# Turning the keys of batches 2 and 3 by 32x32 block transposes and an exchange through DRAM

## The chip, the core and the metric

The kernel runs on one core of one Trainium2 chip. The metric is the device time of one execution in microseconds (us). Three executions of the kernel before took 861.26 to 861.43 us, with a median of 861.28 us.

## What is computed

A linear attention feeds two pairs of dense layers. All arrays are fp32; there are 4 batches, 8 heads, 576 positions and 64 channels a head, so 2304 tokens of 512 channels, and 2048 hidden channels in each of the two layers.

```python
q_s = softmax of q over the channels of a head      # (4, 8, 576, 64)
k_s = softmax of k over the 576 positions
kv  = np.einsum('bhsd,bhse->bhde', k_s, v)          # 64 x 64 per head
x   = np.einsum('bhsd,bhde->bhse', q_s, kv)         # -> (2304, 512)
h   = x @ moe_w_in;   x = elu(h) @ moe_w_out
h   = x @ moe2_w_in;  out = (h * tanh(softplus(h))) @ moe2_w_out
```

The sum over positions in `kv` does not depend on the order of the positions, as long as K and V are in the same order.

## The kernel before

Matrix products are made of three fp32r products of high and low parts, so that a step of the first layer has 12 matmuls for the hidden channels (`mm_h`, L409) and 12 for the output (`mm_y`, L458). The 2304 tokens are 18 tiles of 128, worked through in five blocks `j` of 4, 3, 4, 3 and 4 tiles; a block has 16 **slots** `f`, one for each 128 of the hidden channels. In a slot TensorE does `mm_h(j, f)` and then `mm_y` of two slots before; ScalarE and VectorE make the ELU and the split into parts in between. A block of 3 tiles has matmuls of 384 columns, one of 4 tiles has 512.

The attention of the next tokens is laid beside these slots, by a table of entries `at(j, f, where, function)`. Within a slot the places stand in a fixed order: "load" (DMA issues), the ELU's exponentials, "mid", the ELU's join on VectorE, then "pe" (on TensorE that is right behind `mm_h` and ahead of `mm_y`), "post", "last" and "late". Every engine, and every DMA queue, works through its own instructions in the order of this table; an instruction that waits holds up all behind it on the same engine. Nearly all loads go through the queue of SyncE (SP), stores of split weights through GpSimd's (POOL).

`kv_chain(j, f, b)` (from L606) places the keys and values of batch `b`, four pairs `hp` of heads, each pair at slot `s = f + 2 hp`. Batch 1 runs beside block 0, batch 2 beside block 1 and batch 3 beside block 2; for the latter two `f` is -1, so pairs 0 to 3 have s = -1, 1, 3 and 5. For a pair: `load_k` fetches K with the 128 channels of the pair on the partitions and 576 positions along them (L218); `k_max` (VectorE, L241) and `k_exp` (ScalarE, L248) make the exponentials in place. For `kv` the positions have to lie on the partitions. `k_turn` does this with four 128x128 transposes on TensorE (L263), `k_turn_rest` with one for the last 64 positions (L280); `k_turned` and `k_turned_rest` copy them out of PSUM with ScalarE (L268, L286). `load_v` fetches V (L225, and L229 for the last 64 rows) into one buffer that all pairs share, `k_kv` multiplies (L297; five chunks of positions, two heads each), and `k_scale` writes the result, divided by the sums, into `kvbd`. There it is used by `q_x` (L369) for the query tiles, which are prepared in the same way by `q_chain`.

Three buffers hold K (tag `kT`); the third query tile of a block borrows one. A DMA on SP's queue also waits for the eighth DMA ahead of it, since eight completion counters are used in turn.

Of the kernel before, what the change touches and what calls it, by code (L numbers as in the profile page):

```python
# [8 lines left out]
F32 = mybir.dt.float32  # L9
# [7 lines left out]
P = 128  # L17
# [23 lines left out]
def attention_elu_mish(  # L41
# [15 lines left out]
    nc = tc.nc  # L57
    B, DM, S = kT.shape
    NT = q.shape[0]
    DFF = w1_in.shape[1]  # L60
    D = 64
    NHP = DM // P
# [18 lines left out]
    NC = (S + P - 1) // P  # L81
# [6 lines left out]
    dram = ctx.enter_context(tc.tile_pool(name="dram", bufs=1, space=bass.MemoryType.DRAM))  # L88
# [117 lines left out]
    km_t, qm_t, kv_t, turn_t, x_t = {}, {}, {}, {}, {}  # L206
# [14 lines left out]
    def load_v(b, hp, t=None):  # L221
        if t is None:
            t = ap.tile([P, NC, P], F32, tag="v", name="v", bufs=1)
        full = S // P
        nc.sync.dma_start(  # L225
            out=t[:, 0:full, :], in_=v[b, hp, 0:full * P, :].rearrange("(c p) e -> p c e", p=P)
        )
        if S % P:
            nc.sync.dma_start(out=t[0:S % P, full, :], in_=v[b, hp, full * P:S, :])  # L229
            nc.gpsimd.memset(t[S % P:P, full, :], 0.0)  # L230
        v_t[b, hp] = t
# [19 lines left out]
    def inverse(s):  # L251
        nc.vector.tensor_scalar(out=s, in0=s, scalar1=EPS, scalar2=None, op0=ALU.add)
        nc.vector.reciprocal(out=s, in_=s)
# [34 lines left out]
            )  # L288

    def k_kv(b, hp, ps=None):  # L290
        e, vv = en_t.pop((b, hp)), v_t.pop((b, hp))
        if ps is None:
            ps = att_psum()
        for c in range(NC):

            for a in (0, D):
                nc.tensor.matmul(  # L297
                    out=ps[a:a + D, a:a + D], lhsT=e[:, c, a:a + D], rhs=vv[:, c, a:a + D],
                    start=(c == 0), stop=(c == NC - 1),
                )  # L300
        kv_t[b, hp] = ps

    def k_scale(b, hp, engine=None):
        ps, r = kv_t.pop((b, hp)), rk_t.pop((b, hp))
        for h in range(2):
            a, z = h * D, (h + 1) * D
            to, by = kvbd[b % 2][a:z, hp, a:z], r[a:z, :]
            if engine is None:
                nc.scalar.activation(out=to, in_=ps[a:z, a:z], func=AF.Copy, scale=by)
            else:  # L310
                engine.tensor_scalar(
                    out=to, in0=ps[a:z, a:z], scalar1=by, scalar2=None, op0=ALU.mult
                )

    NH = DM // D

# [281 lines left out]
    def at(j, f, where, fn, *a):  # L598
        j, f = j + f // NF, f % NF
        beside.setdefault((j, f, where), []).append((fn, a))  # L600
# [5 lines left out]
    def kv_chain(j, f, b):  # L606
        for hp in range(NHP):

            s = f + 2 * hp
            if j or hp > 2:  # L610
                at(j, s - 2, "load", load_k, b, hp)
            if (b, hp) not in v_t:
                at(j, s + 2, "load", load_v, b, hp)
            at(j, s, "late", k_max, b, hp)
            at(j, s, "late", k_exp, b, hp)
            at(j, s + 2, "post", lambda b, hp: inverse(rk_t[b, hp]), b, hp)
            at(j, s + 3, "post", k_scale, b, hp)


            rest = s + 1 if j else s + 2  # L620
            if j and hp:
                at(j, s + 1, "pe", k_kv, b, hp - 1)
            at(j, rest, "pe", k_turn_rest, b, hp)
            at(j, rest, "pe", k_turned_rest, b, hp)
            if not j or hp == NHP - 1:
                at(j, s + 3, "pe", k_kv, b, hp)
            at(j, s + 1, "pe", k_turn, b, hp)
            at(j, s + 1, "pe", k_turned, b, hp)

# [271 lines left out]
```

## Time and profile before

| | |
|---|---|
| median of three executions | 861.28 us (861.26 to 861.43) |
| span of the profiled execution, first to last instruction | 859.0 us |
| time outside that span, against the median | 2.3 us |
| TensorE busy (matmuls) | 849.1 us, 99% of the span |
| VectorE / ScalarE / GpSimd busy | 587.7 / 456.4 / 160.6 us |
| DMA, mean over the span | 114 GB/s |

The profiled execution is known by its span alone: its own time is not among the three. Busy time of TensorE is not work at peak, since matmuls overlap; the pace of the starts in the timeline tells what one costs. The whole stretch that the change touches lies between about 120 and 260 us, beside blocks 1 and 2.

### The profile page before, as it was taken

Reading aid. Unit: us, or ns where it says so; the run is one execution under the profiler, and the core shown is the slowest. Engines: PE = TensorE matmul, PEld = TensorE weight load, DVE = VectorE, ACT = ScalarE, POOL = GpSimd, SP = SyncE. Lnnn points to the kernel's source line nnn. Section 1 sums busy time; section 2 is a strip of 40 time slices with the busy share of each in tenths; the row PEclk is TensorE's granted clock in tenths of the full one; section 3 lists DMA queues with packets and bytes.
Section 4 is the critical chain, followed back from the end, with each engine's and each line's share of the span. In section 5 each row is a group of like instructions: output and inputs, shape, how many; then the busy total and the mean of one; then the engine's idle time right before and its main releaser. Section 6 shows DMA issues by size and latency. Waiting matters only on the chain.

```text
span 859.0 us, 11796 instructions
## 1 busy us (share of the span) xinstructions
PE 849.1 (99%) x4408; PEld 734.4 (86%) x4408; DVE 587.7 (68%) x1040; ACT 456.4 (53%) x865; POOL 160.6 (19%) x210
## 2 busy tenths in 40 slices
PE   8999999999999999999999999999999999999998
PEld 5778889998888899988889998888888888888996
DVE  7899856655455367444446878777777777777776
ACT  7897757656554465544444544444444444444443
POOL 4365623223211233223332000000000000000000
PEclk9999999999999999999999999999999999999999
DMA  9791547553643374437977003100210021000101
GB/s 307 244 320 51 185 128 262 163 152 97 215 137 98 112 220 117 136 104 235 290 238 266 1 1 98 38 1 1 98 50 1 1 74 50 1 1 0 50 1 38
DMA packets 55050, 98.30 MB, mean 114 GB/s; under 512 B 3920, under 2 KB 32848, under 8 KB 52432
## 3 DMA queue, kind: packets, MB, share of 16 engines
q1 hardware_dynamic: 38720, 52.31, 19.8%
q0 software_dynamic: 16128, 45.09, 16.0%
q8 instruction: 35, 0.57, 0.3%
q14 instruction: 23, 0.19, 0.1%
q10 hardware_dynamic: 144, 0.13, 0.0%
HBM read 70.25 MB, written 27.26 MB: 114 GB/s over the span
## 4 chain that ended last, share of the span: by engine, by line
PE 95%; ACT 1%; issue 1%; POOL 1%; DVE 1%; DMA 0%; SPq 0%; POOLq 0%; ACTq 0%
PE h L409 44%; PE y L458 23%; PE y L546 15%; PE a L546 8%; PE a L369 2%; PE a L297 1%; PE a L355 1%; PE a L263 1%; DMA q<-in_q_dram 0%; POOL wil L186 0%; PE a L280 0%; DVE qs L340 0%; ACT early L148 0%; ACT woh L180 0%; POOL wol L186 0%
## 5 line engine op out<-in xcount | busy, mean ns | idle before, releaser
L424 DVE SCALAR_TENSOR_TENSOR e<-h,e 128x512 f32<-128x512 f32 (+1 forms) x80 | 50.9, 637 | 116.9 <-ACT e L420 116.5
L409 PE MATMUL h<-xha,wih 128*128 128x512 f32 (+1 forms) x328 | 125.1, 385 | 0.7 <-ACT xha L385 0.7
L409 PE MATMUL h<-xla,wih 128*128 128x512 f32 (+1 forms) x328 | 125.3, 385 | 0.5 <-DVE xla L389 0.5
L409 PE MATMUL h<-xha,wil 128*128 128x512 f32 (+1 forms) x328 | 125.3, 385 | 0.3 <-POOL wil L186 0.3
L514 ACT ACTIVATE r<-n,two 128x512 f32<-128x512 f32 (+1 forms) x80 | 54.6, 683 | 131.3 <-DVE n L510 131.3
L458 PE MATMUL y<-gh,wol 128*128 128x512 f32 (+1 forms) x320 | 120.7, 379 | 0.3 <-POOL wol L186 0.3
L458 PE MATMUL y<-gh,woh 128*128 128x512 f32 (+1 forms) x320 | 117.5, 369 | 0.0
L458 PE MATMUL y<-gl,woh 128*128 128x512 f32 (+1 forms) x320 | 117.4, 368 | 0.0
L416 ACT ACTIVATE e<-h 128x512 f32<-128x512 f32 (+1 forms) x80 | 44.5, 556 | 119.4 <-PE h L409 119.4
L409 PE MATMUL h<-xhb,wih 128*128 128x384 f32 (+1 forms) x304 | 104.8, 345 | 0.0
L409 PE MATMUL h<-xhb,wil 128*128 128x384 f32 (+1 forms) x304 | 104.7, 344 | 0.0
L409 PE MATMUL h<-xlb,wih 128*128 128x384 f32 (+1 forms) x304 | 104.6, 344 | 0.0
L186 POOL TENSOR_TENSOR lo<-raw,hi 128x512 fp32r<-128x512 f32 x32 | 44.2, 1380 | 234.1 <-ACT hi L180 130.9
L493 ACT ACTIVATE u<-h 128x512 f32<-128x512 f32 (+1 forms) x80 | 44.1, 552 | 71.6 <-PE h L409 71.6
L503 DVE TENSOR_SCALAR u<-u 128x512 f32<-128x512 f32 (+1 forms) x80 | 32.0, 400 | 65.0 <-ACT u L493 65.0
L442 DVE TENSOR_TENSOR gl<-e,gh 128x512 fp32r<-128x512 f32 (+1 forms) x80 | 52.5, 656 | 33.6 <-ACT gh L438 33.5
L546 PE MATMUL y<-woh,gl 128*128 128x512 f32 x192 | 75.3, 392 | 0.0
L546 PE MATMUL y<-woh,gh 128*128 128x512 f32 x192 | 75.2, 391 | 0.0
L546 PE MATMUL y<-wol,gh 128*128 128x512 f32 x192 | 74.8, 389 | 0.0
L409 PEld LDWEIGHTS h<-xha,wih 128*128 128x128 f32 x328 | 61.1, 188 | 13.1 <-ACT xha L385 0.9
L409 PEld LDWEIGHTS h<-xha,wil 128*128 128x128 f32 x328 | 61.2, 188 | 12.8 <-POOL wil L186 0.8
L409 PEld LDWEIGHTS h<-xla,wih 128*128 128x128 f32 x328 | 61.2, 188 | 12.6 <-DVE xla L389 0.7
(164 smaller groups left out, 1749.0 us busy)
## 6 DMA issues: line engine op xcount, KB each, us to landing
raw<-in_moe_w_out_dram SPq DMA_DIRECT2D x23, 512.0 KB, 4.7
raw<-in_moe_w_in_dram SPq DMA_DIRECT2D x21, 512.0 KB, 5.0
early<-in_moe_w_in_dram SPq DMA_DIRECT2D x11, 512.0 KB, 5.9
early<-in_moe_w_out_dram SPq DMA_DIRECT2D x9, 512.0 KB, 6.4
out_dram<-o SPq DMA_DIRECT2D x17, 256.0 KB, 2.3
w2ih<-hi POOLq DMA_DIRECT2D x16, 256.0 KB, 4.8
w2il<-lo POOLq DMA_DIRECT2D x16, 256.0 KB, 5.2
w2oh<-hi POOLq DMA_DIRECT2D x16, 256.0 KB, 5.1
```

Of the source, the lines that this page charges most:

```text
L186: nc.gpsimd.tensor_tensor(out=lo, in0=z, in1=hi.bitcast(F32), op=ALU.subtract)
L263: nc.tensor.transpose(out=ps[:, c], in_=k_t[b, hp][:, c], identity=ident)
L369: nc.tensor.matmul(out=ps[:, hp, t0:t1], lhsT=kvbd[b % 2][:, hp, :], rhs=u[:, hp, t0:t1], start=True, stop=True,)
L409: nc.tensor.matmul(out=h_t[f][:, c], lhsT=w[:, i, k * P:(k + 1) * P], rhs=x[k][:, c], start=(n == 0), stop=(n == 3 * KD - 1),)
L416: nc.scalar.activation(out=e, in_=h_t[f], func=AF.Exp)
L424: nc.vector.scalar_tensor_tensor(out=e, in0=h_t[f], scalar=0.0, in1=e, op0=ALU.max, op1=ALU.subtract)
L442: nc.vector.tensor_tensor(out=gl_t[f], in0=h_t.pop(f), in1=gh_t[f].bitcast(F32), op=ALU.subtract)
L458: nc.tensor.matmul(out=y_t[e][:, 0:gh.shape[1]], lhsT=w[:, i, e * P:(e + 1) * P], rhs=x, start=(f == 0 and n == 0), stop=(f == NF - 1 and ...
L493: nc.scalar.activation(out=u, in_=h_t[f], func=AF.Exp)
L503: nc.vector.tensor_scalar(out=u, in0=u, scalar1=U_MAX, scalar2=None, op0=ALU.min)
L514: nc.scalar.activation(out=r, in_=n, func=AF.Ln, bias=two)
L546: nc.tensor.matmul(out=y_t[p, t], lhsT=x[:, c], rhs=w[:, i, :], start=(f == 0 and n == 0), stop=(f == NF - 1 and n == 2),)
```

## The change

For batches 2 and 3 (`b > 1`, that is j = 1 and 2 in `kv_chain`) the transposes on TensorE and the copies on ScalarE are gone. In their place the exponentials are written to DRAM as they lie (`k_out`, one DMA of 128 runs of 2304 bytes) and read back by `k_in` in another arrangement: four DMAs to 32 partitions each, in runs of 512 bytes, and two in runs of 128 bytes for the last 64 positions. In the new arrangement each 32x32 block has its channels on the partitions, and blocks that belong to one range of positions share a partition group; VectorE then transposes all blocks in place (`k_blocks`, two instructions, 128x4x4x32 and 128x128). After it a partition holds four neighbouring positions instead of positions 128 apart, so V is read in the same order ("(p c) e": 128 runs of 2048 bytes instead of 512 runs of 512). `k_kv` reads the turned K with its 64 channels 16 bytes apart for four of its five chunks (`k_heads`). The slots of the table move: `load_v` from s+2 to s+4, `k_kv` from s+3 (where the next pair's entry is at its s+1) to s+5, `k_scale` from s+3 to s+5. The batches 0 and 1 are untouched.

```diff
@@ load_v
+        rows = "(p c) e -> p c e" if b > 1 else "(c p) e -> p c e"
         nc.sync.dma_start(
-            out=t[:, 0:full, :], in_=v[b, hp, 0:full * P, :].rearrange("(c p) e -> p c e", p=P)
+            out=t[:, 0:full, :], in_=v[b, hp, 0:full * P, :].rearrange(rows, p=P)
         )
@@ k_kv
-                    out=ps[a:a + D, a:a + D], lhsT=e[:, c, a:a + D], rhs=vv[:, c, a:a + D],
-                    start=(c == 0), stop=(c == NC - 1),
+                    out=ps[a:a + D, a:a + D],
+                    lhsT=k_heads(b, hp, c, a) if b > 1 else en_t[b, hp][:, c, a:a + D],
+                    rhs=vv[:, c, a:a + D], start=(c == 0), stop=(c == NC - 1),
                 )
@@ new functions
+    R = 32
+
+    def k_out(b, hp):
+        d = dram.tile([P, S], F32, name=f"turn_k{b}{hp}")
+        nc.sync.dma_start(out=d, in_=k_t[b, hp])
+        turn_t[b, hp] = d
+
+    def k_in(b, hp):
+
+        t, n = en_t[b, hp].rearrange("p c e -> p (c e)"), S // P * P
+        d = turn_t.pop((b, hp)).rearrange("(a j) s -> j a s", j=R)
+        for to, size, first in ((t[:, 0:n], P, 0), (t[:, n:n + P], R, n)):
+            for r in range((S - first) // size if first else P // R):
+                nc.sync.dma_start(
+                    out=to[r * R:(r + 1) * R, :].rearrange("j (a s) -> j a s", s=size),
+                    in_=d[:, :, first + r * size:first + (r + 1) * size],
+                )
+
+    def k_blocks(b, hp):
+        t, n = en_t[b, hp].rearrange("p c e -> p (c e)"), S // P * P
+        for x in (t[:, 0:n].rearrange("p (a i c) -> p a c i", i=R, c=n // P), t[:, n:n + P]):
+            nc.vector.transpose(out=x, in_=x)
+
+    def k_heads(b, hp, c, a):
+        t, n = en_t[b, hp].rearrange("p c e -> p (c e)"), S // P
+        if c < n:
+            t = t[:, 0:n * P].rearrange("p (a j c) -> p c a j", j=R, c=n)[:, c]
+        else:
+            t = t[:, n * P:].rearrange("p (a j) -> p a j", j=R)
+        return t[:, a // R:(a + D) // R, :]
@@ kv_chain
-                at(j, s + 2, "load", load_v, b, hp)
+                at(j, s + (4 if j else 2), "load", load_v, b, hp)
@@
+            if j:
+                at(j, s + 1, "late", k_out, b, hp)
+                at(j, s + 2, "late", k_in, b, hp)
+                at(j, s + 4, "post", k_blocks, b, hp)
+                at(j, s + 5, "pe", k_kv, b, hp)
+                at(j, s + 5, "post", k_scale, b, hp)
+                continue
             at(j, s + 3, "post", k_scale, b, hp)
-            rest = s + 1 if j else s + 2
-            if j and hp:
-                at(j, s + 1, "pe", k_kv, b, hp - 1)
-            at(j, rest, "pe", k_turn_rest, b, hp)
-            at(j, rest, "pe", k_turned_rest, b, hp)
-            if not j or hp == NHP - 1:
-                at(j, s + 3, "pe", k_kv, b, hp)
+            at(j, s + 2, "pe", k_turn_rest, b, hp)
+            at(j, s + 2, "pe", k_turned_rest, b, hp)
+            at(j, s + 3, "pe", k_kv, b, hp)
```

The order that the table gives is seen best at two places. (Line numbers in the rows of the change are those of the changed file: L298 there is L297 here, L443 is L409, L492 is L458, L226 and L230 are L225 and L229, L237 is L236.) First TensorE in block 1, slot 2, between `mm_h` and `mm_y`; `xhb` is the block's input, `kT` the buffer of K, `ident` the identity of a transpose. Before:

```order
L409 MATMUL h<-xhb,wih 128x384
L297 MATMUL a<-v,kT 64x64 x10
L280 MATMUL a<-ident,kT 64x128
L263 MATMUL a<-ident,kT 128x128 x4
L458 MATMUL y_1492<-gh,wol 128x384
```

Of the change, in slot 4, where the same product of pair 0 stands now:

```order
L443 MATMUL h<-xhb,wih 128x384
L298 MATMUL a<-v,kT 64x64 x10
L492 MATMUL y_1468<-gh,wol 128x384
```

The product of a pair stays; the turn of the next pair that stood behind it is gone, and the product stands two slots later.

The second place is SP's queue beside block 1, from the load of V for pair 1 on. Before (the first load of V is that of pair 1, `kT<-in_kT_dram` is K of pair 3):

```order
L225 DMA v<-in_v_dram 128x4x128
L229 DMA v<-in_v_dram 64x128
L218 DMA kT<-in_kT_dram 128x576
L133 DMA raw<-in_moe_w_out_dram 128x1024
L236 DMA q<-in_q_dram 128x512
L225 DMA v<-in_v_dram 128x4x128
```

Of the change, from K of pair 3 to the load of V for pair 1 (`turn_k_1464` is the exchange of pair 1, `turn_k_1587` that of pair 2):

```order
L218 DMA kT<-in_kT_dram 128x576
L331 DMA kT<-turn_k_1464 32x4x128 x4
L331 DMA kT<-turn_k_1464 32x4x32 x2
L133 DMA raw<-in_moe_w_out_dram 128x1024
L322 DMA turn_k_1587<-kT 128x576
L237 DMA q<-in_q_dram 128x512
L226 DMA v<-in_v_dram 128x512
L230 DMA v<-in_v_dram 64x128
```

V of pair 1 was the first DMA behind the product of pair 0 and is now the tenth; K of pair 3, which waits for that same product (its buffer is the one that pair 0 leaves), stands ahead of all the others.

## Rows read from the trace of the kernel before

**Rows 1.** The page: the span, and the busy time of each engine.
```profile
span 859.0 us, 11796 instructions
...
PE 849.1 (99%) x4408; PEld 734.4 (86%) x4408; DVE 587.7 (68%) x1040; ACT 456.4 (53%) x865; POOL 160.6 (19%) x210
```

**Rows 2.** The page: the chain that ended last, by engine.
```profile
PE 95%; ACT 1%; issue 1%; POOL 1%; DVE 1%; DMA 0%; SPq 0%; POOLq 0%; ACTq 0%
```

**Rows 3.** Timeline of TensorE, turn of pair 0; columns: start, us, what, records merged.
```profile
121.30 0.27 PE L280 MATMUL a<-ident,kT 128*64 128x128 f32 x1
121.40 0.60 PE L263 MATMUL a<-ident,kT 128*128 128x128 f32 x4
121.76 0.47 PE L458 MATMUL y<-gh,wol 128*128 128x512 f32 x1
122.07 0.39 PE L458 MATMUL y<-gl,woh 128*128 128x512 f32 x1
```

**Rows 4.** Timeline of TensorE, product of pair 0 and turn of pair 1.
```profile
131.67 0.80 PE L297 MATMUL a<-v,kT 128*64 128x64 f32 x20
132.41 0.30 PE L280 MATMUL a<-ident,kT 128*64 128x128 f32 x1
132.54 0.60 PE L263 MATMUL a<-ident,kT 128*128 128x128 f32 x4
132.90 0.42 PE L458 MATMUL y<-gh,wol 128*128 128x384 f32 x1
```

**Rows 5.** Groups of TensorE by form, 118 to 302 us: count, busy us, mean ns.
```profile
L297 PE MATMUL a<-v,kT 128*64 128x64 f32 x160 | 6.4, 227 | 0.0
...
L263 PE MATMUL a<-ident,kT 128*128 128x128 f32 x32 | 4.8, 273 | 0.0
...
L280 PE MATMUL a<-ident,kT 128*64 128x128 f32 x8 | 2.3, 292 | 0.0
```

**Rows 6.** Timeline of TensorE, fp32 products of the query tiles.
```profile
157.13 1.05 PE L369 MATMUL a<-q,kvbd 128*128 128x128 f32 x8
...
279.61 1.89 PE L369 MATMUL a<-kT,kvbd 128*128 128x64 f32 x16
281.31 0.48 PE L458 MATMUL y<-gh,wol 128*128 128x512 f32 x1
```

**Rows 7.** Groups of ScalarE, 118 to 262 us: every other word read, and all.
```profile
L180 ACT ACTIVATE hi<-raw 128x512 fp32r<-128x512 f32 x13 | 8.5, 654 | 0.0
...
L336 ACT ACTIVATE q<-q 128x512 f32<-128x512 f32 x5 | 3.1, 615 | 0.0
```

**Rows 8.** Groups of VectorE, 118 to 262 us, of the size of a pair's K.
```profile
L241 DVE TENSOR_REDUCE km<-kT 128x1 f32<-128x576 f32 x8 | 5.9, 736 | 0.0
L330 DVE TENSOR_TENSOR q<-q,qm 128x512 f32<-128x512 f32 x5 | 3.7, 745 | 0.2
```

**Rows 9.** Timeline of SP's queue behind the products of pairs 0 and 1.
```profile
132.57 0.38 SPq L225 DMA_DIRECT2D v<-in_v_dram  x1
133.00 0.51 SPq L229 DMA_DIRECT2D v<-in_v_dram  x1
133.60 1.40 SPq L218 DMA_DIRECT2D kT<-in_kT_dram  x1
...
142.31 0.38 SPq L225 DMA_DIRECT2D v<-in_v_dram  x1
```

**Rows 10.** V's last rows (L229), issued at 225 us: issue to landing.
```profile
DMA to landing us min/median/max: 2.6/2.6/2.6
```

**Rows 11.** V's last rows (L229), issued at 133 us: issue to landing.
```profile
DMA to landing us min/median/max: 5.6/5.6/5.6
```

**Rows 12.** Loads of K (L218), 90 to 300 us: issue to landing.
```profile
DMA to landing us min/median/max: 4.6/5.5/8.3
```

**Rows 13.** Stretches: busy us of five engines, granted clock, DMA share, GB/s.
```profile
134.00:138.00 4.00, 4.00 (x25) 4.00 (x24) 1.92 (x4) 1.93 (x6) 0.47 (x3) 1.00 1.00 374
...
150.00:154.00 4.00, 4.00 (x41) 3.68 (x40) 3.64 (x7) 3.22 (x9) 1.65 (x4) 1.00 0.47 145
```

More of the change, by code (lines that the diff above doesn't have):

```diff
@@ L290, in k_kv @@
     def k_kv(b, hp, ps=None):
-        e, vv = en_t.pop((b, hp)), v_t.pop((b, hp))
+        vv = v_t.pop((b, hp))
         if ps is None:
@@ L297, in k_kv @@
                 nc.tensor.matmul(
-                    out=ps[a:a + D, a:a + D], lhsT=e[:, c, a:a + D], rhs=vv[:, c, a:a + D],
-                    start=(c == 0), stop=(c == NC - 1),
+                    out=ps[a:a + D, a:a + D],
+                    lhsT=k_heads(b, hp, c, a) if b > 1 else en_t[b, hp][:, c, a:a + D],
+                    rhs=vv[:, c, a:a + D], start=(c == 0), stop=(c == NC - 1),
                 )
+        del en_t[b, hp]
         kv_t[b, hp] = ps
```

## The prediction, made before the change was run

> **What bounds the kernel now.** I read the page first: TensorE is busy for 849.1 of 859.0 us [rows 1], and the chain of work that ended last runs through TensorE for 95% of the span [rows 2]. Busy time alone would not prove a bound, since matmuls overlap, so I went on to the stretches: beside blocks 1 and 2, TensorE never stops and its granted clock is 1.00, the level of 2.4 GHz, while VectorE and ScalarE are idle for a part of nearly every stretch [rows 13]. So in this region a microsecond taken out of TensorE's own order is a microsecond of the end, and a microsecond on another engine or queue counts only if TensorE comes to wait for it. Both have to be worked out: what leaves TensorE's order, and whether the new way of the keys is ready when TensorE asks.
>
> **What leaves TensorE.** Eight pairs (four each of batches 2 and 3) lose their turn: 32 transposes and 8 short ones [rows 5]. Their busy time in these rows overlaps, so I take the starts. Behind a product of keys and values, the turn runs from 132.41 to the next `mm_y` at 132.90, which is 0.49 us [rows 4]; six of the eight pairs stand like that. Pair 0 of each batch has its turn alone: 121.30 to 121.76 is 0.46 us, and the first `mm_y` behind it takes 0.31 instead of the usual 0.23 us (122.07 less 121.76) [rows 3], so 0.54 us. Together 6 x 0.49 + 2 x 0.54 = **4.0 us less**. The product itself stays, at 132.41 - 131.67 = 0.74 us a pair [rows 4], and still has a slot change on either side.
>
> **How the product reads its keys.** It now takes four of five chunks with neighbouring channels 16 bytes apart. No row of before shows that. From below: nothing; a gain is excluded, since the same columns are loaded as before. From above: the product is bound by loading weights, not by its moving columns. The query products show this for fp32: 16 of them with 64 moving columns take 281.31 - 279.61 = 1.70 us, 0.106 us each, and 8 with 128 columns take about 0.11 us each (1.05 us less the 0.27 of the last, over 7) [rows 6]. Both load 128 weight columns. So if loading went at half pace, four fifths of 0.74 us would double: 0.59 us a pair, 4.7 us for eight. The nearest row is a read of every other word: ScalarE takes 654 ns for it against 615 ns for all words [rows 7], 6% more. I take 6% of 4.7, **0.3 us more**, and keep 0 and 4.7 as ends.
>
> A rule speaks against this. The Trainium skill (SBUF — State Buffer, under "Door 1: The DMA port swizzle") says that SBUF is read in lines of 16 bytes, that at least two hits per line are needed to hide the access, and that a read which goes to a new line each time pays. By that rule every channel of the four chunks pays, and the sum is that of the second rival below; by the row, which only steps 8 bytes, it does not.
>
> **What comes onto VectorE.** Two block transposes a pair. From below, half of a pass over a pair's K; from above, twice such a pass. A pass takes 736 or 745 ns [rows 8], so 0.4 to 1.5 us; I take 0.9 us for both (a pass and a quarter of one). The Trainium skill (VectorE: DVE Perf Modes, "The three transpose paths") gives 311 ns for 128x128 in bf16, which for five such squares would be an estimate of 1.6 us. VectorE has the room: a slot pair of block 1 spans about 9.7 us (132.57 to 142.31 between two equal places [rows 9]), and VectorE was idle for 2.1 of 4 us in one stretch and for 0.4 in the next [rows 13], some 2.5 us in 8. The join of the ELU stands ahead of the transposes in their slot. Behind them stand the next pair's maximum, the query tile and the next slot's split, which TensorE wants only a slot later. I cost it at nothing; if the transposes took 2.5 us, the split would be late next. ScalarE loses two copies a pair, which nobody waited for: nothing.
>
> **What comes onto SP's queue.** Per pair one DMA out and six in. `k_out` waits for the exponential, and holds up what stands behind it: K of pair 2, the next weight piece, a query tile, V. `k_in` waits for `k_out` to land. For pairs 0, 2 and 3 there are slots to spare: from the exponential at s to the transposes at s+4 some 17 us pass (two slot pairs less the place within the slot), and the way through DRAM needs two landings of at most 8.3 us [rows 12] or, at the usual 5.5, about 14 us with six issues of 0.5 us. A weight piece is asked for two slots before its use, and the copies that wait for it have a slot to spare. GpSimd's stores of split weights and its memsets keep their places; they share the DMA engines, no more.
>
> Pair 1 is different. Its `k_in` and its V stand behind the load of pair 3's K, and that waits for the product of pair 0, two slots ahead of the product of pair 1. How long does TensorE take from one product's end to the next one's start? Between the two V loads of before lie 9.74 us [rows 9], and these hold one product and turn with its borders, 1.41 us (1.23 us from 131.67 to 132.90, and 0.09 at each side) [rows 4]. That leaves 8.3 us of `mm_h` and `mm_y`; a query tile's four transposes and the border add about 0.5, so **8.9 us**. Now the queue, from the product's end: 0.16 us until SP goes on (132.41 to 132.57), K of pair 3 0.57, six fetches of 0.5 (the 0.51 of the row of 64 partitions), a weight piece, `k_out` and a query tile of 0.4 to 0.6 each, V 0.38, its last rows 0.51, with 0.05 between each two [rows 9]. The last rows of V are issued at 6.1 us and land 2.6 to 5.6 us later [rows 10, 11], at 8.7 to 11.7 us. `k_out` of pair 2 waits, by the count of eight, for K of pair 3, which lands 4.6 to 8.3 us after its issue [rows 12]; at the slow end that adds 4. So TensorE waits for V of pair 1 between 0 and 7 us in block 1. The slow rows fall in a stretch where the DMA engines are full, 1.00 of their time, because of the stores of block 0's outputs [rows 13]; those are over when the product of pair 0 has ended in its new slot, so the fast rows are nearer. I take **1.0 us more** in block 1. The fetches themselves land at 3.7 + 2.6 to 5.6 us, so the transposes end in time or just late. In block 2, with 512 columns a matmul instead of 384, two slots take 8.3 x 512 / 384 = 11.1 us: nothing, with 0 and 5 as ends.
>
> **The sum.** -4.0 + 0.3 + 1.0 = -2.7 us. Made against the profiled span this is 856.3 of 859.0 us; with the 2.3 us that lie outside it, **858.6 us** against the median of 861.28.
>
> **The rivals.** (1) *The keys are read at half pace.* The product goes from 0.74 to about 1.2 us: only the loads grow, and where they were hidden at its borders they stay so; I put 3.7 us for eight in place of 0.3. Then -4.0 + 3.7 + 1.0 = +0.7, **862.0 us**, no change that a measurement can tell. For it speaks that loading is the bound in [rows 6] and that no row has a step of 16 bytes; against it the 6% at a step of 8 bytes [rows 7]. It is what the rule of the Trainium skill cited above (SBUF — State Buffer) would make of this kernel. (2) *SP's queue becomes the bound, and the kernel slower.* In a full stretch a DMA of 128 rows took 1.40 us to issue instead of 0.5 [rows 9]. If the six fetches took 1.2 us each, 4.2 us come onto the chain of pair 1: V's last rows land 4.2 us later in block 1, a wait of 5.2 us, and in block 2 at about 13.5 us against 11.1, a wait of 2.4 us. Then -4.0 + 0.3 + 7.6 = +3.9, **865.2 us**. It decides from a fetch of about 0.9 us on. For it: 56 more DMAs on one queue, and a chain without a slot to spare; against it, that the DMA engines are half idle there (0.47 [rows 13]). (3) *Nothing of the wait comes true and reading is free:* -4.0, **857.3 us**; that is the low end of my own case. That the turns don't leave TensorE is no rival: the order shows them gone.
>
> **The numbers.** My case, 857.2 to 860.3 us, has 0.53; the first rival, 860.5 to 863, 0.27; the second 0.18; 0.02 is left for what I have not seen. A measurement of this kernel tells about 0.2%, 1.7 us. Of my case a part with waits of 2 to 3 us falls within that, 0.08: faster 0.46 (with the remainder of 0.01), same 0.08 and most of the first rival, 0.33, slower 0.21 with its tail, in which both costs meet. The range leaves out the second rival: 857.2 to 863.0.
>
> **What would show each step.** In the timeline of TensorE the products of pairs 0 to 3 should stand alone in slots 4, 6, 8 and 10 of blocks 1 and 2, each of about 0.75 us; 1.2 us says rival 1. Ahead of the product of pair 1 in block 1 a gap of about 1 us, ended by the landing of V's last rows; none in block 2. Six fetches of 0.5 us each on SP's queue; 1.2 us says rival 2. Two transposes on VectorE of 0.9 us together, with no idle time ahead of them. I am wrong if the span is above 860.7 us with the products at 0.75 us and gaps under 1 us, since then time went to a place that I have not named.

## The result, and the profile after

The changed kernel takes **868.99 us** (867.65 to 870.17, four executions) where the kernel before takes 861.27 us: 1.0089 times as long, with a 95% interval of 1.0075 to 1.0103. It is slower by 7.7 us, and outside the predicted range.

The page of the changed kernel, its span, busy times and the chain that ended last by engine (these answer to [rows 1, 2]):

```profile
span 867.2 us, 11845 instructions
...
PE 851.2 (98%) x4368; PEld 734.8 (85%) x4368; DVE 598.3 (69%) x1056; ACT 451.9 (52%) x849; POOL 160.7 (19%) x210
...
PE 91%; DMA 3%; issue 1%; ACT 1%; SPq 1%; POOL 1%; DVE 1%; POOLq 0%; DVEq 0%; ACTq 0%
```

Forty instructions have left TensorE, and yet its busy time has grown by 2.1 us; and DMAs, 0% of the chain before, are now 3% of it.

Where in the program does the time lie? The first `mm_h` of blocks 1, 2 and 3 starts at 119.19, 198.32 and 295.03 us in the kernel before and at 120.01, 204.63 and 303.27 us in the changed one. So block 1 takes 84.62 instead of 79.13 us (**+5.5**), block 2 98.64 instead of 96.71 (**+1.9**), and what lies ahead of block 1, where nothing was changed, 0.8 us more. These make up the 8.2 us between the spans. TensorE's timeline in block 1, ahead of the query tile's turn and around the product of pair 1, and in block 2 around the product of pair 1 (answers to [rows 4]; L298 is the product, L389 a query tile's turn):

```profile
146.00 0.34 PE L443 MATMUL h<-xhb,wih 128*128 128x384 f32 x1
146.78 0.63 PE L389 MATMUL a<-ident,q 128*128 128x128 f32 x4 [0.45 <-DVE q L379]
...
151.24 0.34 PE L443 MATMUL h<-xhb,wih 128*128 128x384 f32 x1
154.42 1.29 PE L298 MATMUL a<-v,kT 128*64 128x64 f32 x20 [2.84 <-DMA v<-in_v_dram]
155.65 0.45 PE L492 MATMUL y<-gh,wol 128*128 128x384 f32 x1
...
240.40 0.39 PE L443 MATMUL h<-xha,wih 128*128 128x512 f32 x1
242.32 1.29 PE L298 MATMUL a<-v,kT 128*64 128x64 f32 x20 [1.53 <-DMA kT<-turn_k]
243.54 0.50 PE L492 MATMUL y<-gh,wol 128*128 128x512 f32 x1
```

Two things are to be seen. The product lasts 155.65 - 154.42 = 1.23 us where it lasted 0.74 [rows 4], and so do all eight. And TensorE stands still three times: 0.6 us ahead of a query tile's turn, 2.9 us for V of pair 1 in block 1 (3.18 from start to start, less the usual 0.27), and 1.6 us in block 2. The last is again V: the transposes had ended at 238.6 us (they start at 237.29 and take 1.30), while V's last rows, issued at 236.21, took 5.9 us to land, to 242.1. The profile names a fetch instead, but those of pair 1 had landed by 237.3 us, and those of pair 2 landed from 243.5 us on, when the product had long begun.

Behind the long wait the clock falls. Stretches of 1 us in the changed kernel (start and end, sum, then busy time and count of TensorE, weight loads, VectorE, ScalarE and GpSimd, granted clock, DMA share, GB/s):

```profile
155.00:156.00 1.00, 1.00 (x16) 0.93 (x15) 0.90 (x3) 0.76 (x2) 0.20 (x1) 1.00 0.64 144
156.00:157.00 1.00, 1.00 (x6) 1.00 (x5) 1.00 (x3) 0.37 (x2) 0.00 (x0) 0.59 0.67 61
157.00:158.00 1.00, 1.00 (x5) 1.00 (x5) 0.90 (x3) 0.00 (x0) 0.00 (x0) 0.50 0.85 281
158.00:159.00 1.00, 1.00 (x5) 1.00 (x4) 0.69 (x1) 0.00 (x0) 0.00 (x0) 0.50 1.08 401
159.00:160.00 1.00, 1.00 (x6) 1.00 (x5) 0.00 (x0) 0.53 (x1) 0.00 (x0) 0.70 1.04 402
```

At 0.50, the level of 1.2 GHz, matmuls start every 0.32 instead of 0.174 us. From 155.93 to 159.94 us 15 of them start; 14 steps at 0.174 are 2.44 us, so this costs 4.01 - 2.44 = 1.6 us.

SP's queue behind the product of pair 0, block 1, and GpSimd's order at the same time (answers to [rows 9]):

```profile
142.01 0.34 SPq L218 DMA_DIRECT2D kT<-in_kT_dram  x1
142.39 2.80 SPq L331 DMA_DIRECT2D kT<-turn_k  x6
145.29 0.41 SPq L133 DMA_DIRECT2D raw<-in_moe_w_out_dram  x1
145.80 0.38 SPq L322 DMA_DIRECT2D turn_k<-kT  x1
146.22 0.45 SPq L237 DMA_DIRECT2D q<-in_q_dram  x1
146.76 0.71 SPq L226 DMA_DIRECT2D v<-in_v_dram  x1
147.52 1.00 SPq L230 DMA_DIRECT2D v<-in_v_dram  x1
```

```profile
142.04 0.15 POOL L216 MEMSET kT<- 64x64 f32 x1 [7.35 <-PE a L298]
142.27 1.72 POOL L186 TENSOR_TENSOR lo<-raw,hi 128x512 fp32r<-128x512 f32 x1
143.93 0.57 POOL L189 DMA_DIRECT2D w2oh<-hi  x1
144.50 0.53 POOL L190 DMA_DIRECT2D w2ol<-lo  x1
```

K of pair 3 goes out 0.1 us behind the end of the product of pair 0 (141.90), and all of pair 1 behind it: V is the eleventh DMA behind that product (not the tenth, as said ahead of the prediction), and its last rows go out 5.6 us later. Their landing (the answer to [rows 10, 11]):

```profile
DMA to landing us min/median/max: 6.7/6.7/6.7
```

GpSimd waits for the same product, in the memset that belongs to that load of K, and 512 KB of split weights behind it (L189, L190) go out just ahead of V.

### The profile page after: what moved, and what is told of

Read it like the earlier page. It is cut to its first block, busy times and chain, and to the rows that moved or that the text cites. A ratio compares the mean times of both kernels' runs of the same rounds, so it can differ in the third digit from the quotient of the medians.

```text
span 867.2 us, 11845 instructions
## 1 busy us (share of the span) xinstructions
PE 851.2 (98%) x4368; PEld 734.8 (85%) x4368; DVE 598.3 (69%) x1056; ACT 451.9 (52%) x849; POOL 160.7 (19%) x210
## 4 chain that ended last, share of the span: by engine, by line
PE 91%; DMA 3%; issue 1%; ACT 1%; SPq 1%; POOL 1%; DVE 1%; POOLq 0%; DVEq 0%; ACTq 0%
PE h L443 43%; PE y L492 22%; PE y L580 15%; PE a L580 7%; PE a L403 2%; PE a L298 1%; DMA early<-in_moe_w_in_dram 1%; DMA v<-in_v_dram 1%; PE a L389 1%; DMA turn_k<-kT 1%; DMA early<-in_q_dram 1%; SPq L331 0%; POOL wil L186 0%; PE a L264 0%; SPq L218 0%
## 5 line engine op out<-in xcount | busy, mean ns | idle before, releaser
L443 PE MATMUL h<-xha,wih 128*128 128x512 f32 (+1 forms) x328 | 125.0, 385 | 0.7 <-ACT xha L419 0.7
L458 DVE SCALAR_TENSOR_TENSOR e<-h,e 128x512 f32<-128x512 f32 (+1 forms) x80 | 50.9, 636 | 108.2 <-ACT e L454 107.7
L443 PE MATMUL h<-xla,wih 128*128 128x512 f32 (+1 forms) x328 | 125.2, 385 | 0.3 <-DVE xla L423 0.3
L443 PE MATMUL h<-xha,wil 128*128 128x512 f32 (+1 forms) x328 | 125.1, 385 | 0.3 <-POOL wil L186 0.3
L492 PE MATMUL y<-gh,wol 128*128 128x512 f32 (+1 forms) x320 | 121.5, 381 | 0.3 <-POOL wol L186 0.3
L492 PE MATMUL y<-gh,woh 128*128 128x512 f32 (+1 forms) x320 | 118.0, 370 | 0.0
L492 PE MATMUL y<-gl,woh 128*128 128x512 f32 (+1 forms) x320 | 117.9, 370 | 0.0
L443 PE MATMUL h<-xhb,wil 128*128 128x384 f32 (+1 forms) x304 | 104.8, 345 | 0.0
L443 PE MATMUL h<-xhb,wih 128*128 128x384 f32 (+1 forms) x304 | 104.7, 344 | 0.0
L443 PE MATMUL h<-xlb,wih 128*128 128x384 f32 (+1 forms) x304 | 104.5, 344 | 0.0
L472 ACT ACTIVATE gh<-e 128x512 fp32r<-128x512 f32 (+1 forms) x80 | 47.0, 588 | 54.7 <-PE y L492 48.2
L443 PEld LDWEIGHTS h<-xha,wih 128*128 128x128 f32 x328 | 61.1, 188 | 13.1 <-ACT xha L419 0.9
L443 PEld LDWEIGHTS h<-xha,wil 128*128 128x128 f32 x328 | 61.2, 188 | 12.9 <-POOL wil L186 0.9
```

The source lines that it names most:

```text
L443: nc.tensor.matmul(out=h_t[f][:, c], lhsT=w[:, i, k * P:(k + 1) * P], rhs=x[k][:, c], start=(n == 0), stop=(n == 3 * KD - 1),)
L458: nc.vector.scalar_tensor_tensor(out=e, in0=h_t[f], scalar=0.0, in1=e, op0=ALU.max, op1=ALU.subtract)
L472: nc.scalar.activation(out=gh_t[f], in_=h_t[f], func=AF.Copy)
L492: nc.tensor.matmul(out=y_t[e][:, 0:gh.shape[1]], lhsT=w[:, i, e * P:(e + 1) * P], rhs=x, start=(f == 0 and n == 0), stop=(f == NF - 1 and ...
```

## The experiments

Each kernel ran beside the kernel before. The table gives the median, the ratio to before with its 95% interval, and the length of blocks 1 and 2, from the start of the first `mm_h` to the next block's (before: 79.13 and 96.71 us; changed: 84.62 and 98.64). The blocks are those of one profiled execution each, the medians those of 4 to 11 executions. Where TensorE waits, executions of one kernel differ by 2 to 4 us (plain columns 861.42 to 865.66, zeros later 864.23 to 866.25, the changed kernel 867.65 to 870.17), so blocks that differ by less than about 1 us tell nothing by themselves there. The profiled execution of zeros later took 864.23 us, 1.1 below its median, that of the writes by GpSimd 862.24, 1.2 above.

| run | median us | ratio | block 1 | block 2 |
|---|---|---|---|---|
| plain columns | 864.44 | 1.0034 (1.0022 to 1.0046) | 82.05 | 96.87 |
| before, step 16 | 865.28 | 1.0047 (1.0034 to 1.0060) | 81.01 | 98.74 |
| before, step 8 | 861.43 | 1.0001 (0.9992 to 1.0009) | 79.20 | 96.87 |
| K of pair 3 later | 862.06 | 1.0007 (0.9998 to 1.0015) | 79.44 | 97.03 |
| both remedies | 858.35 | 0.9966 (0.9954 to 0.9979) | 77.60 | 95.08 |
| quarter of a fetch | 867.62 | 1.0076 (1.0063 to 1.0089) | 83.92 | 97.85 |
| zeros later | 865.33 | 1.0052 (1.0038 to 1.0066) | 81.82 | 97.03 |
| runs of 64, V early | 862.78 | 1.0019 (1.0010 to 1.0028) | 82.16 | 95.22 |
| query tiles ahead | 862.70 | 1.0013 (1.0004 to 1.0022) | 81.48 | 95.23 |
| writes by GpSimd | 861.08 | 0.9997 (0.9988 to 1.0006) | 81.18 | 95.22 |
| one write | 862.09 | 1.0006 (0.9997 to 1.0015) | 82.35 | 95.21 |
| block 2 only | 859.87 | 0.9982 (0.9973 to 0.9991) | 79.14 | 95.21 |

### How the product reads: three runs

The changed kernel with neighbouring columns:

```diff
-                    lhsT=k_heads(b, hp, c, a) if b > 1 else en_t[b, hp][:, c, a:a + D],
+                    lhsT=en_t[b, hp][:, c, a:a + D],
```

> The changed kernel, whose product of keys and values reads 64 neighbouring columns of the turned keys instead of columns 16 bytes apart, in all five chunks; nothing else differs (the channels are then paired with other rows of V, so this run leaves out the right pairing and the output is another). Theory (the step is what makes the product 1.22 us): the product goes back to 0.73 to 0.75 us in all eight places, 8 x 0.49 = 3.9 us less, so about 865.1 us; the waits ahead of the products of pair 1 (3.2 and 1.9 us) stay, since they hang on SP's queue. Rival (the product is long because VectorE's or the DMAs' writes disturb the reads of SBUF, or because it stands alone in its slot): the products stay at 1.2 us and the time at 869 us.

The kernel before with a step, of 16 bytes as here, and of 8 bytes with `"p (h e c) -> p h c e", h=2, c=2` in its place:

```diff
+    def e_cols(e, c, a):
+        e = e.rearrange("p c e -> p (c e)")[:, 0:S // P * P]
+        return e.rearrange("p (e c) -> p c e", c=S // P)[:, c, a:a + D]
@@ k_kv, for b > 1 and c < S // P
-                    lhsT=e[:, c, a:a + D]
+                    lhsT=e_cols(e, c, a)
```

> The kernel before, whose product reads the turned keys of batches 2 and 3 with a step of 16 bytes in four of the five chunks; nothing else differs (wrong columns are paired, so the output is another). Theory: the product goes from 0.73 to about 1.22 us in all eight places, 3.9 us more, 865.2 us, with no wait added and the granted clock at 1.00 throughout. Rival as above (the step is free): 861.3 us.

> The same edit of the kernel before with a step of 8 bytes, so that two of the wanted words lie in each 16 bytes. If the price is one for each line of 16 bytes that gives a single word, and two words a line hide it: 0.74 us a product, 861.3 us. If it goes with the number of lines that a row of weights touches: half the extra, about 0.98 us a product, +2.0, 863.2 us. If any step costs the same: 1.22 us a product, 865.2 us.

All three came out as the theory has it, in the last run the first of its three. The product took 0.73 us with plain columns, 1.22 in the kernel before with the step of 16 bytes, and 0.75 with the step of 8. Here is the product of pair 1 in the kernel before with step 16, from its own start to that of the turn behind it:

```profile
142.28 1.29 PE L301 MATMUL a<-v,kT 128*64 128x64 f32 x20
143.50 0.30 PE L280 MATMUL a<-ident,kT 128*64 128x128 f32 x1
```

The loads of its weights (groups by form: least, median and most ns, over the 160 of batches 2 and 3), in the kernel before with step 16, and with step 8:

```profile
L301 PEld LDWEIGHTS a<-v,kT x160: 136/216/218, 132.1 to 253.7; 128*64 128x64 f32 x160
```

```profile
L301 PEld LDWEIGHTS a<-v,kT x160: 136/138/143, 131.8 to 249.7; 128*64 128x64 f32 x160
```

A load of 64 columns takes 216 ns at a step of 16 bytes and 138 ns at 8. So the step alone costs 3.9 us in the kernel before (865.28 against 861.40 of before beside it), with no wait and no DMA added. The rule of the Trainium skill (SBUF — State Buffer, "Specifications (TRN2)": lines of 16 bytes, at least two hits in each for full bandwidth) says just this, and all three runs agree.

### Who is late, and why: four runs

The changed kernel with one number of the table altered, so that K of pair 3 stands behind the six fetches of pair 1. `load_k` also holds the memset on GpSimd, so this moves both:

```diff
-                at(j, s - 2, "load", load_k, b, hp)
+                at(j, s - (1 if j and hp == NHP - 1 else 2), "load", load_k, b, hp)
```

> The changed kernel with K of pair 3 (blocks 1 and 2) asked for one slot later, so that it stands on SP's queue behind the six fetches of pair 1 instead of ahead of them; its buffer still comes free with the product of pair 0. Theory (SP's queue stands still behind that load until the product of pair 0 has ended, and everything of pair 1 is late by it): the fetches of pair 1 are issued before that product, V of pair 1 some 3 us earlier than the 146.8 us of the changed kernel; the wait of 3.2 us in block 1 falls to 0 to 1 us, that of 1.9 us in block 2 and the 0.5 us ahead of the query tile's turn go, and the clock stays at 1.00 (1.5 us): 6 to 7 us less, 862 to 863.5 us. Products stay at 1.22 us. Rival (the DMA engines are full from 146 to 154 us, and a V asked for earlier lands no earlier): the wait stays at over 2 us and the time at 867 us or more.

It came out at 862.06 us: no wait on TensorE in either block, the clock at 1.00 from 118 to 166 us. The product of pair 1 in block 1 starts 0.26 us behind the last `mm_h`:

```profile
150.43 0.34 PE L443 MATMUL h<-xhb,wih 128*128 128x384 f32 x1
150.69 1.29 PE L298 MATMUL a<-v,kT 128*64 128x64 f32 x20
151.92 0.44 PE L492 MATMUL y<-gh,wol 128*128 128x384 f32 x1
```

SP's queue of this run behind the product of pair 0, which ended at 141.72:

```profile
141.83 0.35 SPq L218 DMA_DIRECT2D kT<-in_kT_dram  x1
142.28 0.39 SPq L133 DMA_DIRECT2D raw<-in_moe_w_out_dram  x1
142.76 0.38 SPq L322 DMA_DIRECT2D turn_k<-kT  x1
143.20 0.50 SPq L237 DMA_DIRECT2D q<-in_q_dram  x1
143.79 0.46 SPq L226 DMA_DIRECT2D v<-in_v_dram  x1
144.31 0.84 SPq L230 DMA_DIRECT2D v<-in_v_dram  x1
```

The six fetches went out from 134.29 us on, and V's last rows at 144.31 instead of 147.52 us; they landed after 5.2 us instead of 6.7. The rival, that a V asked for earlier would land no earlier, falls, though the DMA engines were full at the time (share 1.00 from 142 to 146 us).

Both remedies together, the edits of the first run and of this one:

> Both remedies at once in the changed kernel: neighbouring columns in the product (pairing wrong, output another) and K of pair 3 asked for one slot later. Theory (the two costs are separate and there is no third): 869.0 - 3.9 - 6.9 = 858.2 us, 857.7 to 858.7, products of 0.73 us and no wait on TensorE. Rival (the shorter products leave V less time, so that a wait comes back): a gap ahead of the product of pair 1 and 859 us or more.

858.35 us against 858.2 expected: the two costs are separate. This run has neither, so it shows what the turns were worth: 77.60 and 95.08 us a block, 1.5 and 1.6 us less than before.

What made V land 6.7 us after its issue? Two runs on the changed kernel, the first with

```diff
+                if first == 0:
+                    nc.sync.dma_start(
+                        out=to[r * R:(r + 1) * R, 0:size], in_=d[:, 0, r * size:(r + 1) * size]
+                    )
+                    continue
```

> The changed kernel whose four long fetches of a pair bring only a quarter of their bytes (one block of 32 channels instead of four; the other channels of the product are then unturned exponentials, so the output is another), with the same number of DMAs on SP's queue in the same order. Theory A (V landed 7 us after its issue in block 1 instead of 2.6 to 5.6 because the exchange's own reads fill the DMA engines ahead of it): V lands in about 5 us, the wait of 3.2 us falls below 1.5 us, the clock stays at 1.00, 865 to 866.5 us. Theory B (the engines are filled by what was let go at the same time with them: K, a weight piece, a query tile and the split weights that GpSimd stores late): the fetches are 0.2 of some 2.5 MB, the wait falls by under 1 us, 867.5 to 869 us.

and the second with the memset taken out of `load_k` for pair 3 of batches 2 and 3, and in its place

```diff
+            if j and hp == NHP - 1:
+                at(j, s - 1, "load", k_zeros, b, hp)
```

> The changed kernel with the memset of the zeros in pair 3's K buffer one slot later on GpSimd, its load unchanged. In the changed kernel this memset waits 7.35 us for the product of pair 0 and holds up a split and two stores of split weights (512 KB) behind it, which then fall between 144 and 149 us, just ahead of V. Theory B: these stores go out at about 140 us again, V of pair 1 lands about 1.5 us earlier (512 KB at some 345 GB/s), the wait of 3.2 us falls to 1.5 to 2 us, block 2 keeps its 1.9 us; 865.5 to 867.5 us. Theory A (the exchange itself fills the engines): the wait stays at about 3 us, 868.5 to 869 us.

With a quarter of the bytes, block 1 gained 0.7 and block 2 0.8 us, within what executions differ by, and V's last rows took 6.3 us to land instead of 6.7 in block 1 and 5.3 instead of 5.9 in block 2: the fetches' own bytes are at most a small part of what V waits behind. (With plain columns, which alter no transfer, the landing took 6.0 us in both blocks.) With the zeros later, block 1 gained 2.8 us and block 2 1.6 in the profiled execution (3.7 us by the medians), but not where the expectation put it. In block 1 V still took 5.9 us to land, and the wait for it went only from 2.9 to 2.4 us; what went was the 0.6 us ahead of the query tile's turn and the whole fall of the clock. In block 2, V landed in 4.3 instead of 5.9 us and the wait was gone. So GpSimd's held-up stores account for block 2: it takes 97.03 us here and in the run with K of pair 3 later alike. In block 1 that run is another 2.4 us shorter (79.44 against 81.82; 3.3 us by the medians); this is the rest of the wait, and what the load of K costs by its place on SP's queue. Whether the clock stays up in the other executions of zeros later, of 865.23 to 866.25 us, is not shown.

The 0.6 us have a cause of their own, to be seen on VectorE in the changed kernel:

```profile
142.13 0.69 DVE L161 SCALAR_TENSOR_TENSOR raw<-raw 128x512 uint32<-128x512 uint32 x1
142.74 1.67 DVE L476 TENSOR_TENSOR gl<-e,gh 128x384 fp32r<-128x384 f32 x1
144.33 0.54 DVE L458 SCALAR_TENSOR_TENSOR e<-h,e 128x384 f32<-128x384 f32 x1
```

`gl` takes 1.67 us, and in the run with the zeros later the same instruction takes 0.55. The memset had pushed GpSimd's subtraction (142.27 to 143.99 us) on top of it.

### Towards a version that gains: five runs

The plain columns above pair the wrong rows. A step of 8 bytes can be had with the right ones, if the exchange goes in runs of 64 positions:

```diff
+        d = dram.tile([R, S // G, P // R, G], F32, name=f"turn_k{b}{hp}")    # G = 64
+        for a in range(P // R):
+            nc.sync.dma_start(
+                out=d[:, :, a, :],
+                in_=k_t[b, hp][a * R:(a + 1) * R, :].rearrange("j (k s) -> j k s", s=G),
+            )
@@ k_in
+        for g in range(2):
+            nc.sync.dma_start(
+                out=t[:, g * n // 2:(g + 1) * n // 2],
+                in_=d[:, g * 4:g * 4 + 4].rearrange("j r a s -> r j (a s)"),
+            )
```

In the table, K of pair 3 later as above, and V right behind the product that frees its buffer:

```diff
-                at(j, s + (4 if j else 2), "load", load_v, b, hp)
+                at(j, s + (3 if j else 2), "post" if j else "load", load_v, b, hp)
```

> A version without either cost, if the reading so far is right: the exponentials are written to DRAM in runs of 64 positions (four DMAs, 256 bytes a run), read back by two DMAs of 128 partitions and two short ones, so that the columns of a chunk lie 8 bytes apart instead of 16; K of pair 3 is asked for one slot later and V right behind the product that frees its buffer. Theory: products of 0.75 us, no wait on TensorE in the region, clock 1.00: 861.3 - 4.0 (the turns) + 8 x 0.02 = 857.5 us, 857 to 858.5. Rival (the exchange in runs of 256 bytes loads the DMA engines so much that V or the fetches land late again): a wait ahead of a product of pairs 1 to 3, 859 us or more.

The product took 0.75 us everywhere and block 2 came out at 95.22 us, as hoped. Block 1 did not: TensorE stood 2.9 and 1.9 us (start to start) ahead of a query tile's turns. The rival was right that something is late, but not what: the tile stood on SP's queue behind four writes. Next, that tile ahead of them:

```diff
-        at(j, f - 2, "late", load_q3 if j and o == 2 else load_q, i)
+        at(j, f - 2, "last" if j else "late", load_q3 if j and o == 2 else load_q, i)
```

> The version in runs of 64 positions (8 bytes between columns, K of pair 3 later, V early), with the query tiles of blocks 1 and 2 asked for ahead of the four DMAs that write the exponentials instead of behind them. In the run before it, VectorE waited 3.1 us for a query tile that was issued at 134.3 us behind four writes of 3.8 us together, and TensorE 2.9 us behind it, and 1.9 us once more a slot pair later. Theory (the tile's place on SP's queue): the tile is issued some 4 us earlier, both gaps go: 862.8 - 4.8 = 858.0 us, 857 to 859. Rival (the writes themselves land too late, 9.2 us after their issue in the stretch of the stores of block 0's outputs, so that the transposes stall VectorE and what stands behind them): the gaps shrink by less than half, 860.5 us or more.

And then also the writes on GpSimd's queue:

```diff
@@ k_out
-            nc.sync.dma_start(
+            nc.gpsimd.dma_start(
```

> The same with the four writes of a pair issued by GpSimd instead of SP, ahead of its stores of split weights. Theory: SP's queue gets 2.2 to 3.7 us a pair free, GpSimd has them to spare (busy for 20% of the span); no gap on TensorE, 857 to 858.5 us. Rival (GpSimd's split of a weight piece comes late behind the writes, or its queue is slower): a wait on TensorE or ScalarE for the splits, 859 us or more.

Neither reached its theory: 862.70 and 861.08 us. The query tile's waits were replaced by waits ahead of the product of pair 1, and with the tiles ahead also of pairs 2 and 3. The four writes of pair 1 meet the 2 MB of block 0's outputs, and the fetches go out only at 142 us (142.38 and 142.12). So one write again, as in the changed kernel, and eight fetches of 256-byte runs:

```diff
@@ k_in
+        for r in range(P // R):
+            to = t[r * R:(r + 1) * R, 0:n].rearrange("j (g a s) -> j g a s", g=2, s=G)
+            for g in range(2):
+                k = (g * 4 + r) * G
+                nc.sync.dma_start(out=to[:, g], in_=d[:, :, k:k + G])
```

> As the run with the query tiles ahead, but the exponentials of a pair go to DRAM in one write of 128 runs of 2304 bytes, as in the changed kernel, and come back in eight fetches of 32 partitions in runs of 256 bytes and two short ones. In the two runs before it, the four writes of pair 1 were issued up to 134 us, into the stretch of the stores of block 0's outputs, and landed at 142 us, so that the transposes and what stands behind them on VectorE, or V, came late: gaps of 2.0, 1.0 and 1.2 us in block 1, none in block 2. Theory (the one write is out before these stores, as in the run with K of pair 3 later, where the first fetch went out at 134.3 us): no gap, products of 0.75 us, 857 to 858.5 us. Rival (ten fetches a pair, of 0.5 to 1.4 us issue each, fill SP's queue, and V or a query tile comes late): a gap in block 1 again, 859.5 us or more.

Here the rival held (862.09 us): pairs 0 to 2 were in time, but the ten fetches of pair 3 kept SP's queue from 162.33 to 167.92 us, and V behind them landed too late. SP had stood still ahead of them, until the write of pair 3, issued at 157.88, had landed at 162.31; which of the two made V late was not separated.

```profile
171.37 0.34 PE L450 MATMUL h<-xhb,wih 128*128 128x384 f32 x1
173.02 0.70 PE L301 MATMUL a<-v,kT 128*64 128x64 f32 x16 [1.31 <-DMA v<-in_v_dram]
174.41 0.46 PE L301 MATMUL a<-v,kT 128*64 128x64 f32 x4 [0.68 <-DMA v<-in_v_dram]
```

In all four of these runs block 2 took 95.2 us without a gap. Hence the last run, the four writes and the query tiles ahead, for batch 3 alone:

```diff
@@ kv_chain, and `b > 2` for `b > 1` in k_kv and load_v
-            if j:
+            if j > 1:
                 at(j, s + 1, "late", k_out, b, hp)
```

> The version with four writes and the query tiles ahead, for batch 3 (beside block 2) alone; batch 2 keeps its turn on TensorE as in the kernel before. Theory (block 2's exchange was ready in time in the last two runs, without a gap): half the turns go, 4 x 0.49 = 2.0 us less, 4 x 0.02 more: 861.3 - 1.9 = 859.4 us, 858.9 to 860. Rival (the gain in block 2 is given back elsewhere): 861 us or more.

859.87 us, 0.9982 of before (0.9973 to 0.9991). It is 1.4 us faster than the kernel before, 0.2%: block 1 as before (79.14), block 2 1.5 us shorter. A version that gains in block 1 too was not found; with the queues as they are, each order tried left one transfer late there.

## Why the prediction was wrong

It forecast 858.6 us from a sum of -2.7; measured was +7.7. By its terms, with the blocks of the table, -3.2 for the turns, +3.8 for the read, +5.2 for waits in block 1 and +1.6 in block 2 make 7.4 us; with the 0.8 us ahead of block 1 this is the 8.2 us between the profiles.

- **The turns, -4.0: mis-sized, -3.2.** They left TensorE as forecast (block 1 -1.53, block 2 -1.63 in the run with both remedies). The rest is nearly all in slot 2, and the profile puts it down to cover that was lost. There the product and the next turn used to stand between `mm_h` and `mm_y` [rows 4], and now nothing does; the first `mm_y` of a block writes PSUM that VectorE is still reading for the block before. In that run slot 2 takes 4.57 us in block 1 and 5.76 in block 2 (from its first `mm_h` to the next), where slot 3, also with nothing laid into it, takes 4.16 and 5.44: 0.7 of the 0.8 us. Block 2 in that run (L492 is `mm_y`, L502 the reader, four of 0.49 us):

```profile
209.90 0.39 PE L443 MATMUL h<-xha,wih 128*128 128x512 f32 x1
210.28 0.50 PE L492 MATMUL y<-gh,wol 128*128 128x512 f32 x1
210.62 0.40 PE L492 MATMUL y<-gl,woh 128*128 128x512 f32 x1
210.85 0.39 PE L492 MATMUL y<-gh,woh 128*128 128x512 f32 x1
```

```profile
209.67 1.95 DVE L502 TENSOR_TENSOR xlb<-y,xhb 128x384 fp32r<-128x384 f32 x4 [1.31 <-ACT xhb L501]
```

  The steps from 209.90 on are 0.38 and 0.34 us instead of 0.23. Among those that waited for L502 the profile has the weight loads of `mm_y`, here 0.4 us, and in block 1 0.2:

```profile
  PEld y L492: 0.4, 1
```

  In the run with block 2 only, slot 2 of block 2 is as long (5.77), and slot 2 of block 1, where the turn stands as before, is as before (5.62). A run that changes the reader alone was not made.

- **The strided read, +0.3: the step that failed first.** "The nearest row is a read of every other word" [rows 7] was taken as the price. It was the wrong neighbour: a step of 8 bytes is all but free for the loads too, and one of 16 is not. Measured +3.8 (the run with K later less the one with both remedies: 1.84 and 1.95), as the first rival had it (3.7), from [rows 6] and the bound of loads at half pace: 0.49 us a pair, where half pace in full would be 0.59. (Where the prediction says that by the rule of lines "the sum is that of the second rival below", it is the first that it means.)

- **V of pair 1 in block 1, +1.0: wrong in the landing.** The chain on SP's queue was worked out well: V's last rows at 5.6 us behind the product, forecast 6.1. "The fast rows are nearer" was the error: they landed after 6.7 us, above both rows shown [rows 10, 11]. Much was let go with them at once, by SP and GpSimd, but what of it made the landing long in block 1 was not separated: it took 6.3 us with a quarter of the fetches, 5.9 with GpSimd's stores out of the way, and 6.0 with plain columns, which alter no transfer. With K of pair 3 later, V was issued 3.2 us earlier and landed after 5.2 us. The wait cost 2.9 us, and with it came what had no term: the clock, 1.6, and the query tile's turn, 0.6. Together 5.1 of the 5.2 us that block 1 lost to waits (84.62 less 79.44).

- **Block 2, "nothing": 1.6 us.** The span between the products was as forecast (11.1 us), V's issue 6.6 us behind the first; a landing of 5.9 us was enough to miss it.

- **"GpSimd's stores of split weights and its memsets keep their places": true of the order, false of the time.** The memset of pair 3's buffer is tied to the same product as its load, and waited 7.35 us; the zeros-later run shows what hung on it: 3.7 us by the medians, 4.4 in the profiled execution.

- **VectorE's transposes, nothing: right.** They took 1.3 us a pair instead of 0.9 and delayed nothing by themselves: the run with K later has them all, and no gap. The one of 128x512 takes 1.1 us and the one of 128x128 0.3; the estimate from the bf16 figure of the Trainium skill (VectorE: DVE Perf Modes, "The three transpose paths"), 1.6 us, was nearer than mine. (The two stretches of [rows 13] from which VectorE's room was taken are not neighbours; over the five from 134 to 154 us VectorE was idle for 5.8 of 20 us, about as much.)

- **The second rival** had the right side and nearly the right cost of the waits (7.6 us; measured 6.8 with the clock), but by another cause, so this was luck: the six fetches took 2.80 us together in block 1, 0.47 each, and 3.87 in block 2, not 1.2 each.

The two costs met, which the prediction had named only as a tail. What lies ahead of block 1, 0.8 us longer in the profile of the changed kernel and 0.2 to 1.0 in those of the other runs, is not explained.

## What to carry to other kernels

Price a strided read of weights by the step in bytes, and not by the nearest read that happens to be strided: two fp32 words apart was all but free here, four words apart made the product two thirds longer. When a consumer is moved later, list every queue whose next instruction waits for the buffer that it frees: here one moved product held up a load on SP and a memset on GpSimd, and a number in the table that put both behind the work that didn't need the buffer gave back 6.9 us. And do not price a landing by the row of a calm stretch: V's last rows took 2.6 us there and 6.7 behind all that was let go together.

## What the runs showed of the hardware

- The step counts on VectorE as well. Its transposes read their blocks with the step that the product reads later: 16 bytes in the changed kernel, 8 in the version in runs of 64 (groups of each by line; least, median and most ns over both shapes, so the most is the shape of 128x512; the order of the blocks differs too):

```profile
L339 DVE STREAM_TRANSPOSE kT<-kT x16: 268/712/1144, 138.2 to 266.1; 128x512 f32<-128x512 f32 x8, 128x128 f32<-128x128 f32 x8
```

```profile
L351 DVE STREAM_TRANSPOSE kT<-kT x16: 260/482/704, 137.9 to 260.0; 128x512 f32<-128x512 f32 x8, 64x128 f32<-64x128 f32 x8
```

  1.14 against 0.70 us: with 8 bytes the shape of 128x512 costs no more than a plain pass over a pair's K [rows 8].

- The fall of the clock followed waits of TensorE, but not every wait. Waits here are from start to start. The granted clock fell to 0.50, the level of 1.2 GHz, after two waits with 4.5 us between them in the changed kernel (0.8, then 3.2 us), with plain columns (1.1, then 2.3) and with the quarter of a fetch (0.8, then 2.5), after a single one of 2.3 us with the writes on GpSimd's queue (0.50 from 153 to 155 us) and after two close together with one write (1.7, then 1.4; 0.50 from 175 to 177 us). It stayed at 1.00 after a single one of 2.6 us with the zeros later, after 2.9 and, some 11 us later, 1.9 us in the first version in runs of 64, and in block 2 after single ones of 1.9 us in the changed kernel and 2.1 with plain columns. What decides is open.
- VectorE's subtraction with two inputs took 1.67 instead of 0.55 us while GpSimd's, also with two, took 1.72 instead of 1.31. The Trainium skill (SBUF — State Buffer, "SBUF: two separate sides") says that the two share a pair of ports under an exclusive lock, held for a whole instruction. The times come near to a lock, without proving one: VectorE's began at 142.74 us and ended at 144.41, 0.42 us behind the end of GpSimd's at 143.99, where by a strict lock all of its 0.55 us would follow; and the first 0.55 us of GpSimd's lay beside VectorE's L161, which has two inputs as well.
